# First product of seven experts: seven products of quarters in place of eight (Strassen), with the turned rows copied by two engines

## The chip, the cores and the metric

The kernel runs on one core of one Trainium2 chip. The core has five engines that run side by side and wait for each other through semaphores: TensorE (PE; the loads of its stationary operand are shown as PEld), the vector engine (DVE), the scalar engine (ACT), GpSimd (POOL) and SyncE (SP), which here only starts transfers. The metric is the time of the device for one execution, in microseconds. The kernel before takes 585.48 us (median of three runs, 585.11 to 586.97). One execution was profiled; its span, from the first to the last instruction, is 578.5 us.

## The reference

An attention block feeds a block of eight experts. Inputs are fp32, and so is all arithmetic. Only the second block is touched by the change:

```python
def _moe_ref(x, expert_emb, tau, w1, w2):         # x: 3072 x 512
    ...
    expert_idx = np.argmax(logits, axis=1)        # one of 8 experts per row
    ...
    for e in range(E):
        mask = expert_idx == e
        h = np.maximum(x[mask] @ w1[e], 0.0)      # w1[e]: 512 x 1024
        out[mask] = gate_w[mask, None] * (h @ w2[e])   # w2[e]: 1024 x 512
    return out
```

So each expert has a first product (512 by 1024), a ReLU, a second product (1024 by 512) and a factor for each row. How many rows an expert gets is known only when the kernel has computed the router.

## The kernel before

The attention part and the router take about the first 220 us. They end with tables in memory that say, for each expert, which rows are its own. What follows is the expert stage, eight rounds of `expert` called from the main function, written out for e = 0 to 7. The order of instructions on every engine is that of the program: the code asks for a manual schedule on all engines.

An expert is handled transposed. `load_rows` reads the row numbers (`emt`), casts them on DVE (`ids`, L877) and gathers up to 512 rows with GpSimd (`xg`, L881). `turn_rows` transposes them on TensorE, 16 transposes of 128 x 128 in four groups, each group into one bank of the pool `work`; DVE copies each group to `xT` (L895). `xT` holds 4 blocks of the 512 inner elements, with the rows of x along its free axis.

The number of rows is rounded up to one of 13 widths w (128, then 160 to 512 in steps of 32). For each width the code has a copy of the work, an "arm", and `tc.Switch` sends every engine to its arm by a branch (the Switch is at L957). The branch comes once per expert and engine. Ahead of it `take_width` has loaded the index into each engine's registers (L1002).

In an arm, the first product (L968) goes through the 8 blocks of 128 hidden elements, two at a time into the two banks of a tile of the pool `big` (two such tiles). Each block takes 4 matmuls, one per inner block, with a 128 x 128 piece of w1 as the stationary operand and w columns of `xT` moving. ACT applies the ReLU to both banks at once and writes them to `hT` (L970). Then `turn_rows` transposes the rows of the next expert, and the second product follows: `second` for each full group of 128 rows (L904, 16 records in the profile, 8 matmuls in the code; a bank of `work`), `second_part` for a remainder of 64 or 32 rows (L939). DVE scales each result with the gate into `y` (L907, L942) and GpSimd scatters it to the output. The group 0 comes last, outside the arm, into a bank of its own (`work0`); so TensorE has work while the engines leave an arm and reach the next one.

Weights: two sets of buffers alternate. SyncE starts w1 of expert e+1 when the first product of expert e−1 is over, and its w2 when the second product of expert e−1 is over, which is when expert e begins. The first 256 rows of expert 0 are handled during the attention part, so that expert 0 has only 160 columns left in this stage. Experts 1 to 7 have 320, 512, 320, 352, 384, 480 and 384 columns.

Of the kernel before, what the change touches and what calls it, by code (L numbers as in the profile page):

```python
# [9 lines left out]
F32 = mybir.dt.float32  # L10
# [10 lines left out]
P = 128  # L21
# [867 lines left out]
def turn_rows(k, rows, xT):  # L889

    for j, xg in enumerate(rows[2]):
        ps = k.work.tile([P, k.NC, P], F32, name="work", tag="work")
        for c in range(k.NC):
            k.nc.tensor.transpose(ps[:, c, :], xg[:, c * P : (c + 1) * P], k.ident[:])  # L894
        k.nc.vector.tensor_copy(out=xT[:, :, j * P : (j + 1) * P], in_=ps[:])  # L895


def second(k, rows, hT, w2, j, pool):

    nc = k.nc  # L900
    mt, ids, _ = rows
    ps = pool.tile([P, k.DM], F32, name="work", tag="work")
    for f in range(k.NF):
        nc.tensor.matmul(ps[:], lhsT=hT[:, f, j * P : (j + 1) * P], rhs=w2[:, f, :],  # L904
                         start=f == 0, stop=f == k.NF - 1)
    y = k.yp.tile([P, k.DM], F32, name="y", tag="y")
    nc.vector.tensor_scalar_mul(y[:], ps[:], mt[:, j, 2:3])  # L907
    nc.gpsimd.indirect_dma_start(  # L908
        out=k.out[:, :], out_offset=bass.IndirectOffsetOnAxis(ap=ids[:, j, 1:2], axis=0),
        in_=y[:], in_offset=None, bounds_check=k.N - 1, oob_is_err=False,  # L910
    )


def part_rows(k, rows, base, size):


    nc, mt, n = k.nc, rows[0], P // size
    j, p = base // P, base % P
    ids = k.rp.tile([P, 1], I32, name="pids", tag="pids")
    gate = k.rp.tile([P, 1], F32, name="pgate", tag="pgate")  # L920
    for i in range(n):
        at = slice(i * size, (i + 1) * size)
        nc.vector.tensor_scalar(out=ids[at], in0=mt[p : p + size, j, 1:2], scalar1=float(n), scalar2=float(i),
                                op0=ALU.mult, op1=ALU.add)
        nc.vector.tensor_copy(out=gate[at], in_=mt[p : p + size, j, 2:3])
    return base, size, ids, gate
# [19 lines left out]
    )  # L946


def expert(k, rows, xT, w1, w2, width=None, coming=None, behind=None):


    nc, tc = k.nc, k.tc
    hT = k.hp.tile([P, k.NF, CAP], F32, name="hT", tag="hT")
    if coming:
        coming.xT = k.xtp.tile([P, k.NC, CAP], F32, name="xT", tag="xT")
    arms = [len(WIDTHS) - 1] if width is None else tc.Switch(width.index, len(WIDTHS), hint=width.hint)
    for arm in arms:  # L957
        w = WIDTHS[arm]
        parts = []
        for size in (64, 32):  # L960
            if w % (2 * size) >= size:
                parts.append(part_rows(k, rows, w // (2 * size) * 2 * size, size))
        for f2 in range(k.NF // 2):
            ps = k.big.tile([P, 2, CAP], F32, name="big", tag="big")
            for i in range(2):
                f = 2 * f2 + i
                for c in range(k.NC):
                    nc.tensor.matmul(ps[:, i, 0:w], lhsT=w1[:, c, f * P : (f + 1) * P], rhs=xT[:, c, 0:w],  # L968
                                     start=c == 0, stop=c == k.NC - 1)
            nc.scalar.activation(hT[:, 2 * f2 : 2 * f2 + 2, 0:w], ps[:, :, 0:w], AF.Relu)  # L970
        if coming:
            turn_rows(k, coming.rows, coming.xT)
        for part in parts:
            second_part(k, part, hT, w2)
        for j in range(0 if behind else 1, w // P):
            second(k, rows, hT, w2, j, k.work)
    if coming:
        coming.width = take_width(k, coming.e)
    if behind:
        behind()  # L980
    else:
        second(k, rows, hT, w2, 0, k.work0)
# [16 lines left out]
def take_width(k, e):  # L999

    t = Net()
    v = k.nc.values_load(k.pick[0:1, e : e + 1], engines=ARMS, min_val=0, max_val=len(WIDTHS) - 1)  # L1002
    t.index, t.hint = {eng: v for eng in ARMS}, "expert%d" % e
    k.tc.switch_hint(t.index, len(WIDTHS), t.hint)  # L1004
    return t
# [62 lines left out]
def expert_pools(k, ctx):  # L1068
    def pool(name, bufs):
        return ctx.enter_context(k.tc.tile_pool(name=name, bufs=bufs, reuse_waits="tile"))  # L1070

    k.gp, k.xgp, k.xtp = pool("gp", 3), pool("xgp", 6), pool("xtp", 2)
    k.hp, k.yp, k.rp = pool("hp", 2), pool("yp", 4), pool("rp", 4)


@with_exitstack
def kernel(
    ctx: ExitStack,
    tc: tile.TileContext,
    q: bass.AP,  # L1080
    k: bass.AP,
    v: bass.AP,
    n_global: bass.AP,
    n_local: bass.AP,
    moe_expert_emb: bass.AP,
    moe_tau: bass.AP,
    moe_w1: bass.AP,
    moe_w2: bass.AP,
    out: bass.AP,
):  # L1090
    n = Net()
    n.tc, n.nc = tc, tc.nc
    nc = n.nc
    n.q, n.k, n.v, n.w1, n.w2, n.out = q, k, v, moe_w1, moe_w2, out
    n.emb_in, n.tau = moe_expert_emb, moe_tau
    n.B, n.H, n.S, n.D = q.shape
    n.E, n.DM, n.F = moe_w1.shape
    n.N = n.B * n.S
    n.NT, n.NC, n.NF = n.S // P, n.DM // P, n.F // P
    n.scale = 1.0 / math.sqrt(n.D)  # L1100
    n.slopes = [2.0 ** (-8.0 * (h + 1) / n.H) for h in range(n.H)]
    assert tuple(out.shape) == (n.N, n.DM) and n.DM == n.H * n.D == 512 and n.H == 8
    assert n.D == 64 and n.NT == 6 and n.F % (2 * P) == 0 and n.N % CAP == 0 and n.S == NB * BLK

    n.const = ctx.enter_context(tc.tile_pool(name="const", bufs=1))
    n.x_dram = tc.dram_tile([n.N + 1, n.DM], F32, name="x_dram")
    n.SL = n.N + CAP
    n.ZR = n.N - n.S
    n.meta = tc.dram_tile([n.E * n.SL, 3], F32, name="meta")
    n.c_dram = tc.dram_tile([1, n.E * (n.N // CAP) * 2], I32, name="c_dram")  # L1110
    n.scatters = []

    n.n_global, n.n_local = n_global, n_local
    with ExitStack() as moe:
        wp_a = moe.enter_context(tc.tile_pool(name="wp_a", bufs=1))
        n.w = [new_weights(n, wp_a)]
        def second_weights():
            n.wp_b = moe.enter_context(tc.tile_pool(name="wp_b", bufs=1, side="right", reuse_waits="tile"))
            return n.wp_b

        n.second_weights = second_weights
        n.ea = moe.enter_context(tc.tile_pool(name="ea", bufs=1))
        n.ea2 = moe.enter_context(tc.tile_pool(name="ea2", bufs=FIRST // P))
        with tc.manual_schedule(engines=ORDERED), ExitStack() as inner:
            window_attention(n, inner)

        n.work = ctx.enter_context(tc.tile_pool(name="work", bufs=3, space=PSUM, reuse_waits="tile"))
        n.work0 = ctx.enter_context(tc.tile_pool(name="work0", bufs=1, space=PSUM, reuse_waits="tile"))
        n.big = ctx.enter_context(tc.tile_pool(name="big", bufs=2, space=PSUM, reuse_waits="tile"))
        expert_pools(n, moe)  # L1130

        def prepare(e):
            t = Net()
            t.e = e
            at = e * n.SL
            if e == 0:
                at = nc.values_load(n.si[0:1, 0:1], engines=(SP,), min_val=0, max_val=FIRST)
            t.rows = load_rows(n, n.meta[bass.ds(at, CAP), :], n.gp, n.xgp)
            if e < 2:
                t.w = n.w[e]  # L1140
            else:
                t.w = new_weights(n, (wp_a, n.wp_b)[e % 2])
                load_weights(n, e, t.w)
            return t

        with tc.manual_schedule(engines=ORDERED | set(ARMS)):
            choose_widths(n)
            coming = prepare(0)
            coming.width = take_width(n, 0)
            second(n, n.first.rows, n.first.hT, n.w[0][1], 0, n.work)  # L1150
            coming.xT = n.xtp.tile([P, n.NC, CAP], F32, name="xT", tag="xT")
            turn_rows(n, coming.rows, coming.xT)
            for e in range(n.E):
                now, coming = coming, prepare(e + 1) if e + 1 < n.E else None
                behind = None
                if e == 0:
                    def behind():
                        second(n, n.first.rows, n.first.hT, n.w[0][1], 1, n.work0)
                expert(n, now.rows, now.xT, *now.w, now.width, coming, behind)
    n.scatters = None  # L1160
    leftover(n)

# [27 lines left out]
```

## Time and profile before

| engine | busy, us | share of the span |
|---|---|---|
| PE | 548.2 | 95% |
| PEld | 350.8 | 61% |
| DVE | 164.5 | 28% |
| ACT | 142.3 | 25% |
| POOL | 101.8 | 18% |

| lines | what | records | busy, us |
|---|---|---|---|
| L968 | first product | 512 | 159.0 |
| L904 | second product, full groups | 320 | 139.4 |
| L939 | second product, parts | 320 | 20.4 |
| L894 | transposes of rows | | 2.0 to 2.1 per expert |
| L970 | ReLU on ACT | 32 | 24.9 |
| L895 | copies of turned rows on DVE | 32 | 20.1 |
| L907 | scaling of y on DVE | 22 | 16.5 |

One matmul of the code in fp32 is two records in the profile, each with a load of its stationary operand. A record of TensorE includes its way through the array, so that the mean duration of a record (472 ns for L968) is more than the distance from one start to the next. A line of the timeline gives the start in us from the start of the span, the duration of the merged records in us, engine, line, operation, what is written from what, shape and number of records; in brackets stands the idle time of the engine just before, and what ended it. "issue" there means that the engine waited for nothing that the profile shows. In a line of a table by stretches of time there are, for each engine, busy time and number of records, then the granted clock of TensorE, the share of DMA and its rate.

### The profile page before, as it was taken

To read this page: it belongs to the slowest core of one execution; us is meant where nothing else is said; L and a number is where in the kernel's file an instruction comes from. 1 tells how busy PE (TensorE), PEld (TensorE's weight loads), DVE (VectorE), ACT (ScalarE), POOL (GpSimd) and SP (SyncE) were. 2 spreads that over 40 slices of the span, in tenths; PEclk is the share of its full clock that TensorE was granted. 3 is DMA by queue.
4 is the path that set the end of the run, shared out by engine and by line. 5 is a ranking of instruction groups with operands and counts; after the bars stand their busy time and mean duration, and the time that the engine had idled before them with its cause. 6 is when DMAs were issued, how large, how long until landed. Compare 5 with 4: busy or idle time off the path is not lost.

```text
span 578.5 us, 9188 instructions
## 1 busy us (share of the span) xinstructions
PE 548.2 (95%) x3542; PEld 350.8 (61%) x3542; DVE 164.5 (28%) x411; ACT 142.3 (25%) x336; POOL 101.8 (18%) x130
## 2 busy tenths in 40 slices
PE   8899999999989798999999999999999999999980
PEld 8577788787767676757444447556556444645530
DVE  3254666675775412111000110212101110210010
ACT  4575756756643210001001001001001001001100
POOL 2000015013232225140130013030130130110010
PEclk9799999999989898999999999999999999999995
DMA  8999998994246414543460326443461460010000
GB/s 174 194 186 201 258 254 182 256 235 72 74 128 185 126 25 129 189 150 115 177 238 0 123 84 238 158 142 120 160 232 39 159 226 30 16 43 20 2 36 25
DMA packets 117331, 78.11 MB, mean 135 GB/s; under 512 B 92965, under 2 KB 101157, under 8 KB 117169
## 3 DMA queue, kind: packets, MB, share of 16 engines
q1 hardware_dynamic: 109744, 60.72, 40.9%
q0 software_dynamic: 5536, 15.25, 7.4%
q8 instruction: 51, 0.84, 0.6%
q14 instruction: 112, 0.91, 0.5%
q10 hardware_dynamic: 1888, 0.40, 0.4%
HBM read 63.38 MB, written 13.16 MB: 132 GB/s over the span
## 4 chain that ended last, share of the span: by engine, by line
PE 58%; issue 2%; DMA 1%; POOL 1%; DVE 0%; POOLq 0%
PE big L968 27%; PE work L904 25%; PE work L939 3%; PE work L894 2%; DMA xg<-x_dram,ids 1%; POOL xg L881 0%; POOL out_dram L908 0%; POOL meta L245 0%; DVE y L907 0%; POOLq L1004 0%; DVE flags L1018 0%; POOLq L908 0%; POOLq L881 0%
## 5 line engine op out<-in xcount | busy, mean ns | idle before, releaser
L968 PE MATMUL big<-xT,w1t 128*128 128x320 f32 (+5 forms) x512 | 159.0, 472 | 0.0
L904 PE MATMUL work<-w2t,hT 128*128 128x512 f32 x320 | 139.4, 595 | 0.0
L968 PEld LDWEIGHTS big<-xT,w1t 128*128 128x128 f32 x512 | 95.0, 193 | 64.4 <-issue 31.6
L904 PEld LDWEIGHTS work<-w2t,hT 128*128 128x128 f32 x320 | 60.3, 190 | 74.6 <-issue 73.8
L970 ACT ACTIVATE hT<-big 128x640 f32<-128x640 f32 (+5 forms) x32 | 24.9, 777 | 303.7 <-PE big L968 303.7
L429 DVE TENSOR_TENSOR ex<-ex,table 126x768 f32<-126x768 f32 x64 | 57.7, 904 | 57.9 <-ACT ex L422 55.9
L907 DVE TENSOR_SCALAR y<-work,emt 128x512 f32<-128x512 f32 x22 | 16.5, 751 | 156.7 <-PE work L904 150.0
L422 ACT ACTIVATE ex<-pa 126x384 f32<-126x384 f32 (+1 forms) x128 | 53.3, 476 | 28.8 <-PE pa L418 28.8
L908 POOL DMA_INDIRECT out_dram<-y,ids x22 | 21.8, 992 | 185.6 <-DVE y L907 133.1
L895 DVE COPY xT<-work 128x512 f32<-128x512 f32 x32 | 20.1, 683 | 109.9 <-PE work L894 109.9
L418 PE MATMUL pa<-qT,kT 64*126 64x192 f32 (+1 forms) x512 | 50.7, 336 | 0.4 <-ACT ex L422 0.4
L444 PE MATMUL od<-ex,v 126*64 126x192 f32 (+1 forms) x576 | 48.6, 316 | 0.0
L418 PEld LDWEIGHTS pa<-qT,kT 64*126 64x126 f32 x512 | 41.5, 190 | 10.7 <-issue 6.0
L444 PEld LDWEIGHTS od<-ex,v 126*64 126x64 f32 x576 | 36.0, 142 | 8.8 <-issue 4.7
L881 POOL DMA_INDIRECT xg<-x_dram,ids x34 | 33.3, 981 | 23.0 <-issue 15.6
L245 POOL DMA_INDIRECT meta<-mt,slot x24 | 26.3, 1095 | 38.3 <-DVE good L542 7.8
L452 PE MATMUL od<-ex,halves 126*32 126x192 f32 (+1 forms) x576 | 26.9, 310 | 0.0
L943 POOL DMA_INDIRECT out_dram<-y,pids x7 | 7.1, 1015 | 89.3 <-DVE y L942 84.0
L217 POOL TENSOR_TENSOR ss<-ss,half 128x3 f32<-128x3 f32 (+1 forms) x6 | 6.3, 1047 | 93.0 <-ACT junk L526 93.0
L526 ACT ACTIVATE junk<-xs 128x512 f32<-128x512 f32 x24 | 15.2, 632 | 27.1 <-DVE xs L521 22.2
L939 PE MATMUL work<-w2t,hT 128*32 128x128 f32 (+1 forms) x320 | 20.4, 317 | 0.0
L452 PEld LDWEIGHTS od<-ex,halves 126*32 126x32 f32 x576 | 14.9, 111 | 8.8 <-issue 3.6
(143 smaller groups left out, 389.9 us busy)
## 6 DMA issues: line engine op xcount, KB each, us to landing
w1t<-in_moe_w_dram SPq DMA_DIRECT2D x6, 2048.0 KB, 9.5
w2t<-in_moe_w_dram SPq DMA_DIRECT2D x6, 2048.0 KB, 11.5
v<-in_v_dram SPq DMA_DIRECT2D x32, 192.0 KB, 4.7
x_dram<-xs SPq DMA_DIRECT2D x24, 256.0 KB, 2.8
k<-in_k_dram SPq DMA_DIRECT2D x28, 192.0 KB, 4.0
q<-in_q_dram SPq DMA_DIRECT2D x28, 192.0 KB, 4.2
w1t<-in_moe_w_dram SPq DMA_DIRECT2D x32, 128.0 KB, 3.7
w2t<-in_moe_w_dram SPq DMA_DIRECT2D x32, 128.0 KB, 3.7
```

Of the source, the lines that this page charges most:

```text
L245: i = nc.gpsimd.indirect_dma_start(out=k.meta[:], out_offset=bass.IndirectOffsetOnAxis(ap=slot[:, t : t + 1], axis=0), in_=mt[:, t, :], in ...
L418: nc.tensor.matmul(u.sp[e][0:ROWS, a * n : (a + 1) * n], lhsT=t.kT[rows, j, 0:ROWS], rhs=t.qT[rows, j * BLK : j * BLK + n], start=True, st ...
L422: nc.scalar.activation(u.ex[:, e], u.sp[e][0:ROWS, 0 : 2 * u.n].rearrange("p (a c) -> p a c", a=2), AF.Exp, scale=k.scale)
L429: nc.vector.tensor_tensor(out=exv, in0=exv, in1=tab[:, :, 0 : u.n // BLK, :], op=ALU.mult)
L444: nc.tensor.matmul(g.od[a][e * D : (e + 1) * D, at : at + c1 - c0], lhsT=g.v[0:ROWS, 2 * a + e, u.j, :], rhs=u.ex[:, e, a, c0:c1], start=f ...
L452: nc.tensor.matmul(g.od[2][32 * i : 32 * i + 32, at : at + c1 - c0], lhsT=k.halves[0:ROWS, g.m].rearrange("p i c -> p (i c)"), rhs=u.ex[:, ...
L881: nc.gpsimd.indirect_dma_start(out=xg[:], out_offset=None, in_=k.x_dram[0 : upto or k.N + 1, :], in_offset=bass.IndirectOffsetOnAxis(ap=id ...
L904: nc.tensor.matmul(ps[:], lhsT=hT[:, f, j * P : (j + 1) * P], rhs=w2[:, f, :], start=f == 0, stop=f == k.NF - 1)
L908: nc.gpsimd.indirect_dma_start(out=k.out[:, :], out_offset=bass.IndirectOffsetOnAxis(ap=ids[:, j, 1:2], axis=0), in_=y[:], in_offset=None, ...
L939: nc.tensor.matmul(ps[i * size : (i + 1) * size, 0:m], lhsT=hT[:, f, base : base + size], rhs=w2[:, f, i * m : (i + 1) * m], start=f == 0, ...
L968: nc.tensor.matmul(ps[:, i, 0:w], lhsT=w1[:, c, f * P : (f + 1) * P], rhs=xT[:, c, 0:w], start=c == 0, stop=c == k.NC - 1)
L970: nc.scalar.activation(hT[:, 2 * f2 : 2 * f2 + 2, 0:w], ps[:, :, 0:w], AF.Relu)
```

## The change

For experts 1 to 7, where the width is at least 256, the first product is no longer computed as eight products of quarters (two halves of the inner axis, two of the hidden axis, two of the rows) but as seven, by Strassen's scheme in Winograd's form. With A the quarters of w1, B those of `xT`, the seven left factors are three quarters of w1 and four sums of quarters (`sums`); the right factors are three quarters of `xT` and four differences (`dif`). The seven products, added up in the right way, give the four quarters of the hidden layer. Each product has 8 matmuls of the code with n = w/2 columns. It is done in two halves (`go`), one call of `product` each: 4 matmuls, 8 records of the profile, into one bank, which takes n columns of two hidden blocks. A bank that is used twice accumulates a second product upon the first.

The purpose is fewer columns for TensorE to stream. In return the other engines have more to do:

- DVE makes the four differences of `xT` at the start of the arm (`t1` to `t4`), five sums of a bank and a piece in SBUF for each half (`u2`, `u3` and three that are written to `hT`), and, once per expert, the four sums of the next expert's w1 (`weight_sums`, after the copies of the turned rows and ahead of the gates of the parts).
- ACT copies the first product of each half (`p1`) and applies the ReLU in eight pieces; six of them in place on `hT`, after DVE's sum.
- In `turn_rows` the copies of the groups 1 and 3 go to ACT, for all experts.
- What `second_part` needs of small values (`part_rows`) is computed after the first product instead of ahead of it, when the seven products are used.

```diff
@@ turn_rows
-        k.nc.vector.tensor_copy(out=xT[:, :, j * P : (j + 1) * P], in_=ps[:])
+        eng = k.nc.scalar.copy if j % 2 else k.nc.vector.tensor_copy
+        eng(out=xT[:, :, j * P : (j + 1) * P], in_=ps[:])
@@ new functions
+def weight_sums(k, w1, sums):
...
+    two(0, a(1, 0), a(1, 1), ALU.add)
+    two(1, sums[:, 0], a(0, 0), ALU.subtract)
+    two(2, a(0, 0), a(1, 0), ALU.subtract)
+    two(3, a(0, 1), sums[:, 1], ALU.subtract)
...
+def first_by_seven(k, xT, w1, sums, hT, w):
...
+    t1 = two(0, b(0, 1), b(0, 0))
+    t2 = two(1, b(1, 1), t1)
+    t3 = two(2, b(1, 1), b(0, 1))
+    t4 = two(3, b(1, 0), t2)
...
+    def product(ps, left, right, go, first):
+        for f in range(2):
+            for c in range(K):
+                nc.tensor.matmul(ps[:, f], lhsT=left[:, c, (2 * go + f) * P : (2 * go + f + 1) * P], rhs=right[:, c],
+                                 start=first and f == 0 and c == 0, stop=True, skip_group_check=True)
...
+    one = banks()
+    p1 = [new("p1") for go in range(2)]
+    for go in range(2):
+        product(one[go], a(0, 0), b(0, 0), go, True)
+        nc.scalar.copy(out=p1[go], in_=one[go])
+    for go in range(2):
+        product(one[go], a(0, 1), b(1, 0), go, False)
+        relu(h(0, 0, go), one[go])
+    keep = None
+    for go in range(2):
+        if go == 0:
+            p6, p7 = banks()
+        u2, u3 = new("u2"), new("u3")
+        if go == 1:
+            p6 = keep
+            p7, p5 = banks()
+        product(p6, sums[:, 1], t2, go, True)
+        add(u2, p1[go], p6)
+        product(p7, sums[:, 2], t3, go, True)
+        add(u3, u2, p7)
+        if go == 0:
+            p5, keep = banks()
+        product(p5, sums[:, 0], t1, go, True)
+        add(h(1, 1, go), u3, p5)
+        relu(h(1, 1, go), h(1, 1, go))
+        product(p7, a(1, 1), t4, go, False)
+        add(h(1, 0, go), u2, p7)
+        relu(h(1, 0, go), h(1, 0, go))
+        product(p5, sums[:, 3], b(1, 1), go, False)
+        add(h(0, 1, go), u2, p5)
+        relu(h(0, 1, go), h(0, 1, go))
@@ expert, in the arm
-        parts = []
-        for size in (64, 32):
-            if w % (2 * size) >= size:
-                parts.append(part_rows(k, rows, w // (2 * size) * 2 * size, size))
-        for f2 in range(k.NF // 2):
...
+        if sums is not None and w >= 2 * P:
+            first_by_seven(k, xT, w1, sums, hT, w)
+        else:
+            parts = arm_parts(k, rows, w)
+            first_by_eight(k, xT, w1, hT, w)
         if coming:
             turn_rows(k, coming.rows, coming.xT)
+            weight_sums(k, coming.w[0], coming.sums)
+        if not parts:
+            parts = arm_parts(k, rows, w)
```

`first_by_eight` is the first product as it was. There is one tile `sums` for all experts. Expert 0 gets no sums and keeps the first product of before.

More of the change, by code (lines that the diff above doesn't have):

```diff
@@ L946, in second_part, with arm_parts, first_by_eight @@
     )
-def expert(k, rows, xT, w1, w2, width=None, coming=None, behind=None):
+def arm_parts(k, rows, w):
+    return [part_rows(k, rows, w // (2 * size) * 2 * size, size) for size in (64, 32) if w % (2 * size) >= size]
+def first_by_eight(k, xT, w1, hT, w):
+    nc = k.nc
+    for f2 in range(k.NF // 2):
+        ps = k.big.tile([P, 2, CAP], F32, name="big", tag="big")
+        for i in range(2):
+            f = 2 * f2 + i
+            for c in range(k.NC):
+                nc.tensor.matmul(ps[:, i, 0:w], lhsT=w1[:, c, f * P : (f + 1) * P], rhs=xT[:, c, 0:w],
+                                 start=c == 0, stop=c == k.NC - 1)
+        nc.scalar.activation(hT[:, 2 * f2 : 2 * f2 + 2, 0:w], ps[:, :, 0:w], AF.Relu)
@@ new lines, in new_sums, with a, two @@
+def new_sums(k, pool):
+    return pool.tile([P, 4, k.NC // 2, k.F // 2], F32, name="sums")
+def weight_sums(k, w1, sums):
+    nc, K, M = k.nc, k.NC // 2, k.F // 2
+    def a(m, n):
+        return w1[:, n * K : (n + 1) * K, m * M : (m + 1) * M]
+    def two(i, x, y, op):
+        nc.vector.tensor_tensor(out=sums[:, i], in0=x, in1=y, op=op)
+    two(0, a(1, 0), a(1, 1), ALU.add)
+    two(1, sums[:, 0], a(0, 0), ALU.subtract)
+    two(2, a(0, 0), a(1, 0), ALU.subtract)
+    two(3, a(0, 1), sums[:, 1], ALU.subtract)
@@ new lines, in first_by_seven, with b, two, a @@
+def first_by_seven(k, xT, w1, sums, hT, w):
+    nc, K, M, n = k.nc, k.NC // 2, k.F // 2, w // 2
+    F2 = k.NF // 2
+    dif = k.sp.tile([P, 4, K, CAP // 2], F32, name="dif", tag="dif")
+    def b(i, j):
+        return xT[:, i * K : (i + 1) * K, j * n : (j + 1) * n]
+    def two(i, x, y):
+        nc.vector.tensor_tensor(out=dif[:, i, :, 0:n], in0=x, in1=y, op=ALU.subtract)
+        return dif[:, i, :, 0:n]
+    t1 = two(0, b(0, 1), b(0, 0))
+    t2 = two(1, b(1, 1), t1)
+    t3 = two(2, b(1, 1), b(0, 1))
+    t4 = two(3, b(1, 0), t2)
+    def a(m, i):
+        return w1[:, i * K : (i + 1) * K, m * M : (m + 1) * M]
+    def banks():
+        t = k.big.tile([P, 2, CAP], F32, name="big", tag="big")
+        return [t[:, i, 0:w].rearrange("p (f s) -> p f s", f=2) for i in range(2)]
+    def product(ps, left, right, go, first):
[3 more added lines that the diff above has]
+                                 start=first and f == 0 and c == 0, stop=True, skip_group_check=True)
+    def h(m, j, go):
+        f = m * F2 + 2 * go
+        return hT[:, f : f + 2, j * n : (j + 1) * n]
+    def add(out, x, y):
+        nc.vector.tensor_tensor(out=out, in0=x, in1=y, op=ALU.add)
+    def relu(out, x):
+        nc.scalar.activation(out, x, AF.Relu)
+    def new(name):
+        return k.sp.tile([P, 2, CAP // 2], F32, name=name, tag=name)[:, :, 0:n]
+    one = banks()
[29 more added lines that the diff above has]
+        relu(h(0, 1, go), h(0, 1, go))
@@ L952, in expert @@
+def expert(k, rows, xT, w1, w2, width=None, coming=None, behind=None, sums=None):
     nc, tc = k.nc, k.tc
@@ L959, in expert @@
         parts = []
-        for size in (64, 32):
-            if w % (2 * size) >= size:
-                parts.append(part_rows(k, rows, w // (2 * size) * 2 * size, size))
-        for f2 in range(k.NF // 2):
[L964 to L970, printed above, removed]
+        if sums is not None and w >= 2 * P:
[3 more added lines that the diff above has]
+            first_by_eight(k, xT, w1, hT, w)
         if coming:
             turn_rows(k, coming.rows, coming.xT)
+            weight_sums(k, coming.w[0], coming.sums)
+        if not parts:
+            parts = arm_parts(k, rows, w)
         for part in parts:
@@ L1072, in expert_pools @@
     k.gp, k.xgp, k.xtp = pool("gp", 3), pool("xgp", 6), pool("xtp", 2)
-    k.hp, k.yp, k.rp = pool("hp", 2), pool("yp", 4), pool("rp", 4)
+    k.hp, k.yp, k.rp, k.sp = pool("hp", 2), pool("yp", 4), pool("rp", 4), pool("sp", 2)
 @with_exitstack
@@ L1149 @@
             coming.width = take_width(n, 0)
+            coming.sums, sums = None, new_sums(n, moe.enter_context(tc.tile_pool(name="sums", bufs=1)))
             second(n, n.first.rows, n.first.hT, n.w[0][1], 0, n.work)
@@ L1155 @@
                 behind = None
+                if coming:
+                    coming.sums = sums
                 if e == 0:
@@ L1158, in behind @@
                         second(n, n.first.rows, n.first.hT, n.w[0][1], 1, n.work0)
-                expert(n, now.rows, now.xT, *now.w, now.width, coming, behind)
+                expert(n, now.rows, now.xT, *now.w, now.width, coming, behind, now.sums)
     n.scatters = None
```

## The prediction

> **What bounds the kernel now.** I read the slices of the span first, then the chain that ended last, then TensorE's timeline over the expert stage, and last the vector engine around each start of an expert.
>
> ```profile
> PE   8899999999989798999999999999999999999980
> PEclk9799999999989898999999999999999999999995
> PE 58%; issue 2%; DMA 1%; POOL 1%; DVE 0%; POOLq 0%
> ```
>
> From slice 16 on (230 us) TensorE is busy without a break, at full clock, and the chain runs through it alone: 27% of it is the first product (L968), 25% the second (L904). What TensorE saves there, the kernel saves, if nothing new makes it wait. TensorE's timeline for experts 3 to 7:
>
> ```profile
> 346.73 17.39 PE L968 MATMUL big<-xT,w1t 128*128 128x320 f32 x64
> 383.38 19.10 PE L968 MATMUL big<-xT,w1t 128*128 128x352 f32 x64
> 423.62 20.80 PE L968 MATMUL big<-xT,w1t 128*128 128x384 f32 x64
> 467.01 25.92 PE L968 MATMUL big<-xT,w1t 128*128 128x480 f32 x64
> 520.95 20.80 PE L968 MATMUL big<-xT,w1t 128*128 128x384 f32 x64
> ```
>
> Each of the code's 32 matmuls shows as two records. Experts 1 and 2 have widths 320 and 512, expert 0 has 160. No engine makes TensorE wait inside these products. The vector engine at the start of expert 6 (467.01), from its timeline (start, duration, engine, instruction, idle before):
>
> ```profile
> 467.21 0.75 DVE L907 TENSOR_SCALAR y<-work,emt 128x512 f32<-128x512 f32 x1 [6.12 <-PE work L904]
> 467.88 0.16 DVE L877 CAST ids<-emt 128x8 int32<-128x8 f32 x1
> 473.67 0.14 DVE L923 TENSOR_SCALAR pids<-emt 64x1 int32<-64x1 f32 x1 [5.63 <-issue]
> ```
>
> This is the reading on which all below turns. DVE scales the last rows of the expert before, casts the ids, takes the Switch's branch, and then waits for nothing that the profile shows for 5.63 us before the first instruction of its arm. At 467.2 SyncE starts the 2 MB load of the next w2. At expert 0, with no weight load, the same gap is 2.43 us. Now it costs nothing: DVE has no work for the first product. The records of L957 give DVE's arrival in the arm, after the expert's first matmul: 4.66, 5.35, 6.20, 6.68, 6.09, 6.57 and 3.53 us for experts 1 to 7 (no weights are loaded at the last).
>
> **What the Trainium skill says.** *TensorE: Matmul & The Clock Gate*, Back-to-back issue gap: N/2.4 + 2.5 ns warm. The trace agrees, at two passes a record: expert 0's 160-column records start 136 ns apart from 229 us on (320/2.4 + 2.5), expert 5's 384-column ones 322 ns. The 190 ns that a weight load takes there does not set the pace. *Runtime: NRT & Kernel Launch*, Instruction fetch mechanics: a taken branch to a page that is not held forces a fetch by DMA first. The gaps of 2.43 to 5.75 us marked "issue" after the Switch agree, and grow where the w2 load begins just ahead. *TensorE*, Part 1: after an idle window of some 3.4 us the clock is halved until a busy one. This view (us, busy of PE, PEld, DVE, ACT, POOL, then the clock) agrees:
>
> ```profile
> 220.80:224.20 3.40, 1.28 (x8) 0.84 (x8) 2.27 (x4) 0.00 (x0) 1.02 (x1) 1.00 0.78 202
> 224.20:227.60 3.40, 3.13 (x12) 2.88 (x13) 0.77 (x2) 0.00 (x0) 0.48 (x1) 0.50 0.05 18
> ```
>
> *VectorE: DVE Perf Modes*, errata section: an fp32 tensor_tensor takes (N+151)/0.96 ns; the trace has 549 ns at 384 elements (557 by the formula).
>
> **The change, part by part.** *Products.* 64 records of w columns become 112 of n = w/2. A record costs 2 x columns/2.4 + 2.5 ns, so an expert saves 6.667 ns x w − 0.12 us. Experts 1 to 7 have 320+512+320+352+384+480+384 = 2752 columns: 18.35 − 0.84 = **−17.5 us**. Expert 0 stays.
>
> *The new wait.* The first four calls of product need only xT and w1. They last 32 records: 4.35 us at n=160, 4.77 at 176, 5.20 at 192, 6.48 at 240, 6.91 at 256. The fifth call (p6) needs t2, DVE's second difference, and DVE's differences are the first instructions of its arm. So TensorE stands until arrival + 0.09 (hint to first instruction, as before) + two tensor_tensors of 2n elements + 0.03 (gap of dependent ones, L321 to L322) + 0.06 (DVE's end to TensorE, L895 to L894). The duration is read between the rows of 192 elements (352 ns) and 384 (549): 0.48, 0.52, 0.55, 0.65, 0.68 us. Expert 1: 4.66+0.18+0.97 = 5.81, less 4.35: 1.46 us. Expert 2: 6.89 against 6.91: 0. Expert 3: 7.35 − 4.35 = 3.00. Expert 4: 7.89 − 4.77 = 3.12. Expert 5: 7.37 − 5.20 = 2.17. Expert 6: 8.04 − 6.48 = 1.56. Expert 7: 4.81 against 5.20: 0. Sum **+11.3 us**. Behind the waiting matmul stand all the expert's other products; TensorE runs them in order. I take the arrivals as they are, since branch, fetch and w2 load stay where they were. With an undisturbed fetch at every expert (3.5 us, as at expert 7) the stall is 0.3 us at experts 1, 3 and 4 or less, 1 us in all. With one more line of instructions to be fetched within the longer arm it is some 3 us more.
>
> *Clock.* A stall of 3 us nearly fills a window of 3.4. A halved window costs 3.4/2 = 1.7 us. The trace halves the clock after a window with 1.28 us of TensorE work; slices with 70% and more passed. Experts 3, 4 and perhaps 5 are near the line; I take 1.3 windows, **+2.2 us**, between 0 and five windows (8.5).
>
> *Inside the loop.* A call lasts 8 records, 1.09 to 1.73 us; a sum on DVE 0.5 to 0.7 us plus 0.2 for the signal. Every bank that is reused (p7, p5) has a whole call between its reader and its next matmul, and DVE's five sums in a round take 2.5 to 3.4 us beside 5.4 to 8.6 of TensorE. I price these waits at nothing; so also ACT's copies of p1 and its halved ReLUs (0.44 us at 320 elements from 437 ns): ACT reaches its arm long before TensorE (L957: 453.7 for the expert that starts at 467.0).
>
> *The end of the product.* The last sum and ReLU now come after the last matmul. DVE's add (0.5 to 0.7 us) stands ahead of the copy of the first turned rows, and ACT's ReLU ahead of the second copy. TensorE's fourth group of transposes needs the first copy's bank: copied at 0.2+0.6+0.68 = 1.5 us instead of 1.3 after the product. I take 0.25 us at experts 1 to 6, **+1.5**. Expert 7 has no transposes: its second product runs 4 records (0.87 us) and waits for the last ReLU at 0.2+0.55+0.05+0.5+0.1 = 1.4: **+0.5**.
>
> *Hidden.* weight_sums: four times (1024+151)/0.96 = 1.22 us by the skill's formula, about 5 us on DVE after the copies. Queued behind it are the gates and the scaling of y; TensorE meanwhile has parts and second products of 10 us and more, with three banks, and the sums are wanted an expert later. The next w1 was loaded during the expert before (w1 is issued at 274.21 and 326.32, lands in 9.5 us). ACT's two copies of turned rows cost nothing and bring nothing: they fall into idle time.
>
> Sum: 585.5 − 17.5 + 11.3 + 2.2 + 1.5 + 0.5 = **583.5 us**.
>
> **The rivals.** *DVE in time:* the fetch ends sooner, for instance because the arms lie otherwise in the instruction lines. Then 585.5 − 17.5 + 1 + 2 = **571 us**. Against it: all six middle experts show the gap. For it: 2.4 us at expert 0. *Stalls and clock:* every stall halves a window, five at 1.7 = 8.5 in place of 2.2, and a fetch inside a longer arm adds up to 3: 590 to 593, say **590 us**, slower than before. For it: nothing is known between 1.28 us and about 2.4 us of work in a window. Against it: the window must catch most of the stall. *Weight loads set the pace at half width:* 190 ns a record at n below 226 would add 54, 54, 41, 27.5 and 27.5 ns x 112 at experts 1, 3, 4, 5, 7 = 23 us: **606 us**. Against it: 136 ns measured at 160 columns.
>
> **How the numbers follow.** Forecast as worked out 0.57 (580 to 587 with zero to three halved windows), DVE in time 0.14, stalls and clock 0.26, weight loads 0.03. The likeliest gives 583.5; its neighbours reach from 573, a fetch half as disturbed, to 591. Faster by over 0.3% (below 583.7): the 0.14 and 0.34 of the forecast. Within: 0.20 of it and 0.03 of the third. Slower: the rest.
>
> **What would show it.** TensorE's records of products 160 wide at 136 ns; after 32 records of an expert a gap of 1.5 to 3 us at experts 1, 3, 4, 5, 6, ended by DVE's differences; none at 2 and 7; DVE's "issue" idle of 4 to 6 us ahead of the differences; one or two 3.4 us stretches at clock 0.5 behind those gaps. No gap there would make me wrong towards 571, half clock behind each of them towards 590.

## The result, and the profile after

The changed kernel takes 620.34 us (median of four runs, 618.77 to 623.97), the kernel before on the same chip 585.3 us. The ratio is 1.0603, with a 95% interval of 1.0548 to 1.0658: 35.0 us slower. The forecast was 583.5 us, 2.0 us below the 585.5 it started from, with neighbours from 573 to 591.

First the slices of TensorE and its granted clock over the changed kernel's span (617.4 us), then the shares of its chain of waits:

```profile
PE   9899999979989889979888988988988988997890
PEclk9899999998989899999999999999999999999995
...
PE 52%; issue 4%; DVE 4%; ACT 1%; DMA 1%; POOL 0%; DVEq 0%; POOLq 0%; ACTq 0%
```

In the expert stage the unbroken row of nines has become a row of eights and nines: TensorE is held up a little everywhere and nowhere long. The clock is as full as before (0.978 on average, 0.971 before), so half speed isn't the cause. The chain, which had next to no DVE or ACT work in it (0%), now has 4% of the one and 1% of the other: TensorE waits for them by turns. TensorE's timeline of expert 5, which before was the one line `423.62 20.80`, shows where (L1018 is the matmul of `product`, L1026 the sum on DVE, L1029 the ReLU and L1038 the copy to `p1`):

```profile
447.98 1.46 PE L1018 MATMUL big<-xT,w1t 128*128 128x192 f32 x8
450.06 1.57 PE L1018 MATMUL big<-xT,w1t 128*128 128x192 f32 x8 [0.61 <-ACT p L1038]
452.24 1.57 PE L1018 MATMUL big<-xT,w1t 128*128 128x192 f32 x8 [0.61 <-ACT p L1038]
454.39 1.57 PE L1018 MATMUL big<-xT,w1t 128*128 128x192 f32 x8 [0.58 <-ACT hT L1029]
455.79 1.46 PE L1018 MATMUL big<-dif,sums 128*128 128x192 f32 x8
457.97 2.87 PE L1018 MATMUL big<-dif,sums 128*128 128x192 f32 x16 [0.72 <-issue]
460.68 1.46 PE L1018 MATMUL big<-dif,w1t 128*128 128x192 f32 x8
461.98 1.46 PE L1018 MATMUL big<-xT,sums 128*128 128x192 f32 x8
464.09 2.87 PE L1018 MATMUL big<-dif,sums 128*128 128x192 f32 x16 [0.65 <-DVE hT L1026]
467.60 1.57 PE L1018 MATMUL big<-dif,sums 128*128 128x192 f32 x8 [0.65 <-DVE u L1026]
469.82 1.57 PE L1018 MATMUL big<-dif,w1t 128*128 128x192 f32 x8 [0.65 <-DVE hT L1026]
472.03 1.57 PE L1018 MATMUL big<-xT,sums 128*128 128x192 f32 x8 [0.65 <-DVE hT L1026]
473.43 2.07 PE L894 MATMUL work<-ident,xg 128*128 128x128 f32 x16
```

Eight records are one call of `product`, and at full pace one call starts 8 x 162.5 ns = 1.30 us after the other. That is so at the calls 8 and 9 (460.68 to 461.98), which wait for nothing. Before eight of the fourteen calls (2, 3, 4, 6, 10, 12, 13, 14) TensorE stands, and the call starts 2.1 to 2.2 us after the one before it. The gap that the prediction was about, ahead of the fifth call (455.79), isn't there.

From the first record to the transposes expert 5 takes 473.43 − 447.98 = 25.45 us; at full pace it would be 112 x 162.5 ns = 18.20. So 7.25 us are lost. The same subtraction at experts 1 to 7 gives 6.66, 8.24, 7.44, 7.51, 7.25, 7.99 and 7.25, together 52.3 us. The balance is −17.5 + 52.3 = +34.8 us, and 35.0 were measured. Nothing else of size is left to look for.

Whom does TensorE wait for? The chain of semaphores, summed for its weight loads (idle us, times, longest):

```profile
PEld big L1018 <- DVE hT L1026: 20.1, 21, 1.2
PEld big L1018 <- ACT p L1038: 12.8, 14, 1.1
PEld big L1018 <- DVE u L1026: 12.0, 12, 1.3
PEld big L1018 <- ACT hT L1029: 6.2, 7, 1.1
```

Those are the readers of the banks: DVE's sums (`hT`, `u`) and ACT's copies and ReLUs, three waits for ACT and four or five for DVE in each of seven experts. These figures are idle time of the weight loader, which holds its ordinary pauses too; the losses above are from starts. (Call 6 of expert 5, at 457.97, has "issue" as its releaser; at expert 7, which has the same width, the profile names DVE's `u`.)

Now the second call. It is the clearest case, because it writes into a bank that nothing has used before in this expert. The one instruction of ACT beside it, from ACT's timeline:

```profile
449.53 0.48 ACT L1038 COPY p<-big 128x384 f32<-128x384 f32 x1 [20.18 <-PE big L1018]
```

This copy reads what the first call left in `one[0]`. It ends at 450.01. The second call, into `one[1]`, starts at 450.06. It needs no result of the copy and doesn't touch its bank. What the two banks share is the tile: `banks()` asks the pool for one tile of two banks and hands out slices. All eight waits are of this kind. Call 3 goes into `one[0]`, whose copy ended long ago (450.01), but starts 50 ns after the copy of `one[1]` (451.71 + 0.48 = 452.19); call 6 fills `p7` and waits for the sum that reads `p6`, its neighbour in the tile. The calls without a wait are those in a fresh tile (5, 7, 11) or whose neighbour's reader is done (8, 9).

One such wait costs, at call 2: the way of the last record through the array 0.16, signal 0.09, copy 0.48, signal 0.05: 0.78 us. Later ones cost 0.1 more, since a call that follows a wait is itself longer (1.57 instead of 1.46). Over all widths a wait costs 0.7 us (call 2 of expert 1) to 1.05 us (call 13 of expert 2): the reader has more columns to read there (a copy to `p1` takes 0.42 us at expert 1 and 0.58 at expert 2).

### The profile page after: what moved, and what is told of

It reads as the page before. It is cut to its first block, busy times and chain, and to the rows that moved or that the text cites. A ratio compares the mean times of both kernels' runs of the same rounds, so it can differ in the third digit from the quotient of the medians.

```text
span 617.4 us, 10087 instructions
## 1 busy us (share of the span) xinstructions
PE 545.1 (88%) x3878; PEld 388.9 (63%) x3878; DVE 241.1 (39%) x521; ACT 164.8 (27%) x394; POOL 102.2 (17%) x130
## 4 chain that ended last, share of the span: by engine, by line
PE 52%; issue 4%; DVE 4%; ACT 1%; DMA 1%; POOL 0%; DVEq 0%; POOLq 0%; ACTq 0%
PE work L905 24%; PE big L1018 22%; PE work L940 3%; PE work L894 2%; DVE hT L1026 2%; PE big L963 1%; DVE u L1026 1%; ACT p L1038 1%; DMA xg<-x_dram,ids 1%; ACT hT L1029 0%; DVE dif L1000 0%; POOL xg L881 0%; POOL out_dram L909 0%; POOL meta L245 0%; DVE y L908 0%
## 5 line engine op out<-in xcount | busy, mean ns | idle before, releaser
L1018 PE MATMUL big<-dif,sums 128*128 128x160 f32 (+4 forms) x336 | 62.8, 337 | 15.0 <-DVE u L1026 8.3
L1018 PEld LDWEIGHTS big<-dif,sums 128*128 128x128 f32 x336 | 53.7, 190 | 23.4 <-DVE u L1026 12.0
L1018 PE MATMUL big<-xT,w1t 128*128 128x160 f32 (+4 forms) x224 | 44.0, 339 | 12.7 <-ACT p L1038 8.6
L1029 ACT ACTIVATE hT<-hT 128x320 f32<-128x320 f32 (+4 forms) x42 | 22.3, 531 | 109.3 <-DVE hT L1026 109.3
L1018 PEld LDWEIGHTS big<-xT,w1t 128*128 128x128 f32 x224 | 35.9, 190 | 23.3 <-ACT p L1038 12.8
L1038 ACT COPY p<-big 128x320 f32<-128x320 f32 (+4 forms) x14 | 6.8, 486 | 162.4 <-PE big L1018 162.4
L444 PE MATMUL od<-ex,v 126*64 126x192 f32 (+1 forms) x576 | 49.9, 322 | 0.0
L1026 DVE TENSOR_TENSOR hT<-u,big 128x320 f32<-128x320 f32 (+4 forms) x42 | 23.7, 564 | 51.6 <-PE big L1018 51.6
L1018 PE MATMUL big<-xT,sums 128*128 128x160 f32 (+4 forms) x112 | 21.6, 336 | 4.6 <-DVE hT L1026 4.6
```

What stands on the lines that cost most here:

```text
L444: nc.tensor.matmul(g.od[a][e * D : (e + 1) * D, at : at + c1 - c0], lhsT=g.v[0:ROWS, 2 * a + e, u.j, :], rhs=u.ex[:, e, a, c0:c1], start=f ...
L1018: nc.tensor.matmul(ps[:, f], lhsT=left[:, c, (2 * go + f) * P : (2 * go + f + 1) * P], rhs=right[:, c], start=first and f == 0 and c == 0, ...
L1026: nc.vector.tensor_tensor(out=out, in0=x, in1=y, op=ALU.add)
L1029: nc.scalar.activation(out, x, AF.Relu)
```

## The experiments

The theory after this: the program waits for a tile, not for a bank, and the change is the first code here that gives the two banks of a `big` tile readers of their own. The rival: seven products have true dependencies that cost this in any case (sums that are too slow, banks that are reused too soon). A third reading lays the loss on DVE's and ACT's added work. Two sets of four kernels ran; each set has its own runs of the kernel before (579.70 us median in the first, 587.53 in the second, on two other chips). The second set has the two kernels with the ReLU taken apart, and the late load on the changed kernel and on the kernel before; the first has the other four. So ratios are compared, and "in us of the first chip" is ratio x 585.3.

**One bank to a tile.** The calls, their order and the sums stay. Four tiles of one bank stand in place of two tiles of two. (Expert 0 and the leftover path, which shares the pool, are fitted to this; expert 0's ReLU goes by bank.)

```diff
-        t = k.big.tile([P, 2, CAP], F32, name="big", tag="big")
-        return [t[:, i, 0:w].rearrange("p (f s) -> p f s", f=2) for i in range(2)]
+        t = [k.big.tile([P, CAP], F32, name="big", tag="big") for i in range(2)]
+        return [x[:, 0:w].rearrange("p (f s) -> p f s", f=2) for x in t]
...
-        n.big = ctx.enter_context(tc.tile_pool(name="big", bufs=2, space=PSUM, reuse_waits="tile"))
+        n.big = moe.enter_context(tc.tile_pool(name="big", bufs=4, space=PSUM, reuse_waits="tile"))
```

> The changed kernel with every bank of the first product as a tile of its own (four tiles of one bank in place of two of two banks; the eight-product path applies its ReLU bank by bank). Theory 1 (the waits of the changed kernel are between the two banks of one tile: a matmul into one bank waits for the reader of the other): the gaps of 0.5 to 0.85 us before the calls of product go, 52 us in all; what stays is the wait for DVE's differences, 0 to 3.2 us an expert, 11 us in all. Time 579 to 585 us. Rival A (the chain product, sum, product is itself too slow for two rounds of banks): the gaps stay, 612 us or more. Rival B (the vector engine's added work holds TensorE up): 605 to 620 us.

Measured: 577.32 us, ratio 0.9971 (0.9951 to 0.9991). In us of the first chip that is 583.6. The eight waits are gone. TensorE's timeline of expert 5:

```profile
425.39 5.36 PE L1023 MATMUL big<-xT,w1t 128*128 128x192 f32 x32
433.03 4.17 PE L1023 MATMUL big<-dif,sums 128*128 128x192 f32 x24 [2.28 <-DVE dif L1005]
437.04 1.46 PE L1023 MATMUL big<-dif,w1t 128*128 128x192 f32 x8
438.34 1.46 PE L1023 MATMUL big<-xT,sums 128*128 128x192 f32 x8
439.64 4.06 PE L1023 MATMUL big<-dif,sums 128*128 128x192 f32 x24
443.54 1.46 PE L1023 MATMUL big<-dif,w1t 128*128 128x192 f32 x8
444.84 1.46 PE L1023 MATMUL big<-xT,sums 128*128 128x192 f32 x8
```

The first four calls run as one line of 32 records, the other ten follow each other without a wait, and between the two stands the wait that the prediction had: TensorE for DVE's differences. DVE's timeline there:

```profile
426.26 0.16 DVE L877 CAST ids<-emt 128x8 int32<-128x8 f32 x1
431.83 0.56 DVE L1005 TENSOR_TENSOR dif<-xT 128x384 f32<-128x384 f32 x1 [5.41 <-ACT hT L1034]
432.42 0.56 DVE L1005 TENSOR_TENSOR dif<-xT,dif 128x384 f32<-128x384 f32 x1
```

DVE is idle for 5.41 us between the cast and the first difference. (The releaser named, a ReLU on ACT, writes nothing that the first difference reads: that needs only `xT`, which was copied during the expert before.) Over all experts the waits say:

```profile
PEld big L1023 <- DVE dif L1005: 12.6, 6, 3.2
```

By expert, against full pace, 1.76, 0.66, 6.23, 2.97, 2.55, 1.28 and 0 us are lost, 15.45 in all; −17.5 + 15.45 = −2.0, and the medians differ by −2.4. At expert 3 the loss is not the wait alone. This view by stretches (us, busy of PE, PEld, DVE, ACT, POOL, then the clock) covers it:

```profile
347.00:350.40 3.40, 1.06 (x8) 0.82 (x7) 0.51 (x1) 0.87 (x2) 2.49 (x4) 1.00 0.95 327
350.40:353.80 3.40, 2.80 (x10) 2.80 (x11) 1.51 (x5) 0.00 (x0) 0.44 (x1) 0.50 1.04 410
353.80:357.20 3.40, 3.40 (x14) 3.40 (x14) 0.78 (x2) 0.00 (x0) 0.00 (x0) 0.50 0.48 155
```

After a stretch with 1.06 us of TensorE work the clock is at half for two stretches. In the second of them 14 records fill 3.4 us; at full pace they take 14 x 136 ns = 1.9. The fifth call starts at 351.00, where full pace would have had it at 343.55 + 4.35 = 347.90. So of the 6.23 us 3.1 are the wait and 3.1 are lost behind it, while the clock is at half.

So the eight waits came from the tile: none of them is left. Of the true dependencies only the wait for the differences costs time, which the changed kernel had hidden behind the others. The rival falls. So does the third reading: all of DVE's and ACT's added work is in this kernel too, and its time is that of the kernel before.

**The same readers without the seven products.** If the tile is the cause, the kernel before must show it too as soon as each bank of its tile gets a reader of its own. This takes its one ReLU for two banks apart:

```diff
-        nc.scalar.activation(hT[:, 2 * f2 : 2 * f2 + 2, 0:w], ps[:, :, 0:w], AF.Relu)
+            nc.scalar.activation(hT[:, f, 0:w], ps[:, i, 0:w], AF.Relu)
```

> The kernel before, its products as they were, with the ReLU applied to each bank right after that bank's matmuls, in place of once per tile of two banks. Theory 1 (a matmul into one bank of a tile waits for the reader of its other bank): four waits an expert, each the way through the array plus one ReLU of 0.3 to 0.6 us, 0.6 to 0.95 us in all, over eight experts 26 us: ratio to before 1.040 to 1.048. If the waits of the changed kernel came from the seven products themselves: ratio 0.998 to 1.003.

And this is the same with a tile for each bank (the pool then has four tiles of one bank in place of two of two):

```diff
-        ps = k.big.tile([P, 2, CAP], F32, name="big", tag="big")
         for i in range(2):
+            ps = k.big.tile([P, CAP], F32, name="big", tag="big")
```

> As relu_bank_two, but each bank is a tile of its own. Theory 1: no waits, ratio to before 0.997 to 1.003. If the smaller ReLUs themselves hold TensorE up: the same as relu_bank_two.

Measured: with two banks to a tile 613.81 us, ratio 1.0458 (1.0425 to 1.0491); with one bank to a tile 587.69 us, ratio 1.0000 (0.9983 to 1.0018). TensorE's timeline of expert 5, first with two banks to a tile:

```profile
446.35 2.74 PE L968 MATMUL big<-xT,w1t 128*128 128x384 f32 x8
449.73 5.43 PE L968 MATMUL big<-xT,w1t 128*128 128x384 f32 x16 [0.64 <-ACT hT L970]
455.74 5.43 PE L968 MATMUL big<-xT,w1t 128*128 128x384 f32 x16 [0.58 <-ACT hT L970]
...
467.76 2.85 PE L968 MATMUL big<-xT,w1t 128*128 128x384 f32 x8 [0.58 <-ACT hT L970]
```

and with one:

```profile
430.86 20.80 PE L968 MATMUL big<-xT,w1t 128*128 128x384 f32 x64
```

ReLUs, products and banks are the same in both. The second bank of each tile waits for the ReLU of the first, four times an expert. From start to start 16 records take 6.01 us in place of 16 x 322 ns = 5.16: 0.85 us for a wait. Eight experts with four waits of 0.8 to 0.9 are 26 to 29 us, and 26.3 were measured (613.81 − 587.53). This has nothing of Strassen in it.

**DVE's added work alone.** The differences and the weight sums are made as in the changed kernel, but the first product is then done in eight products of quarters, as before (what DVE has made isn't used):

```diff
     t4 = two(3, b(1, 0), t2)
+    first_by_eight(k, xT, w1, hT, w)
+    return
```

> The changed kernel with the eight products of before; the differences of xT and the sums of w1 are still computed on DVE, but no product uses them; the turned rows are copied in turn. Theory 1: this work lies beside TensorE's, 584 to 588 us. Rival B: a large part of the 35 us stays, 600 us or more.

Measured: 577.84 us, ratio 0.9974 (0.9955 to 0.9993); in us of the first chip 583.8, just under the range expected. DVE's timeline after the turned rows of an expert:

```profile
444.35 1.22 DVE L981 TENSOR_TENSOR sums<-w1t 128x1024 f32<-128x1024 f32 x1
...
451.18 0.75 DVE L908 TENSOR_SCALAR y<-work,emt 128x512 f32<-128x512 f32 x1 [2.08 <-PE work L905]
```

The four sums take 1.22 us each, and DVE is idle for 2.08 us more before TensorE has the first rows to scale. This part of the added work, the differences and the weight sums, is hidden. (The sums of the banks and ACT's smaller pieces aren't in this kernel; they are in the one with one bank to a tile.)

**The turned rows alone**, in the kernel before:

```diff
-        k.nc.vector.tensor_copy(out=xT[:, :, j * P : (j + 1) * P], in_=ps[:])
+        eng = k.nc.scalar.copy if j % 2 else k.nc.vector.tensor_copy
+        eng(out=xT[:, :, j * P : (j + 1) * P], in_=ps[:])
```

> The kernel before with one part of the change: turned rows copied by DVE and ACT in turn. All theories: no effect on TensorE, 584 to 587 us.

Measured: 578.44 us, ratio 0.9981 (0.9967 to 0.9995): 0.2%, less than can be built on.

**Where DVE's late arrival comes from.** The prediction put it on the fetch of the arm's first instructions, slowed by the 2 MB load of w2 that starts at the same moment. The edit on top of one bank to a tile lets this load wait until the rows of the next expert have been gathered (SyncE's next transfer, the 6 KB of row numbers, moves back with it):

```diff
-    nc.sync.dma_start(w[1][:], k.w2[e].rearrange("(f p) m -> p f m", p=P))
+    i = nc.sync.dma_start(w[1][:], k.w2[e].rearrange("(f p) m -> p f m", p=P))
+    for g in after:
+        k.tc.add_manual_dep(i.ins, g.name,
+                            mybir.DependencyInfo(mybir.DependencyClass.Sync, mybir.DependencyReason.DATA),
+                            reason="keeps the transfer away from the branch at an expert's start")
...
-                load_weights(n, e, t.w)
+                load_weights(n, e, t.w, [n.gather.ins])
```

> As one_bank, and the load of the next w2 waits for the last gather of rows, so that it starts some 12 us after an expert's start in place of 0.2 us. If the vector engine's late arrival in its arm comes from its instruction fetch queueing behind that load, it arrives after 3 to 3.6 us at all experts and the wait for the differences falls to about 1 us in all: 569 to 574 us. If the fetch is late for another reason: the time of one_bank within 2 us.

Measured: 562.87 us (560.1 to 566.3), ratio 0.9743 (0.9685 to 0.9801), in us of the first chip 570. DVE's timeline at the start of expert 5 (411.50):

```profile
412.37 0.16 DVE L881 CAST ids<-emt 128x8 int32<-128x8 f32 x1
415.10 0.56 DVE L1009 TENSOR_TENSOR dif<-xT 128x384 f32<-128x384 f32 x1 [2.57 <-ACT p L1047]
```

The w2 load now starts at 424.28, and the idle time after the cast is 2.57 us in place of 5.41. DVE arrives 3.2 to 3.6 us after the first matmul at all seven experts, where it was up to 6.3. The loss against full pace is 0.65 us over all experts; so −17.5 + 0.65 = −16.8 us, and the medians differ by as much (562.87 − 579.70; the runs spread over 6 us, so such closeness is in part chance). This version beats both kernels.

The trace holds more on the fetch than the idle time. In both kernels, at each of the experts 1 to 7, a packet of the DMA queue that the page calls "q14 instruction" starts 1.93 to 2.05 us ahead of the first difference: at expert 5 at 429.87 with the load beside it (difference at 431.83), at 413.13 with the load put off (415.10). Counted from the expert's first matmul it starts after 3.0 to 4.5 us where the load is beside it (experts 1 to 6), and after 1.4 to 1.7 us where none is. The packet itself takes no longer at expert 5 (0.31 and 0.34 us). So if it is the fetch of DVE's first instructions, the delay lies ahead of its start and not in the transfer. The record doesn't name the engine that the packet is for.

The same edit without the other one, on the changed kernel and on the kernel before:

> The changed kernel with two-bank tiles as it is, and the load of the next w2 put off until the last gather of rows has landed. Theory 1: the waits between banks remain and had hidden most of the vector engine's late arrival; only the gaps before the first call with differences go (0.7 us at one expert, 0.5 at another): ratio to before 1.055 to 1.062. If the late fetch were the main cause: below 1.04.

> The kernel before with the load of the next w2 put off in the same way. DVE has nothing to do for the first product there, so all theories: ratio to before 0.998 to 1.002. If putting the load off is worth something by itself (so that the gain of one_bank_w2late isn't that of the seven products): below 0.99.

Measured: 621.57 us, ratio 1.0563 (1.0519 to 1.0608), and 587.71 us, ratio 1.0002 (0.9983 to 1.0022). In the changed kernel DVE now arrives after 3.2 to 3.4 us and the eight waits remain, with their time. In the kernel before nobody waits for DVE's arrival. The late load is worth 13 us (0.9971 to 0.9743) once the tiles are mended, and next to nothing otherwise: a wait that stands behind another one shows its price only when that one is gone.

## Why the prediction was wrong, step by step

**Products, −17.5 us: right.** Records of 160 columns start 136 ns apart. With both waits away, the first products of experts 1 to 7 take 15.39, 24.17, 15.58, 16.81, 18.20, 22.68 and 18.20 us; before it was 17.23, 27.47, 17.23, 18.93, 20.64, 25.76 and 20.64. The difference of the sums is 16.9. The rival of weight loads that set the pace falls.

**"Inside the loop", priced at nothing: this step failed.** It said: "Every bank that is reused (p7, p5) has a whole call between its reader and its next matmul". That is true of the banks, and the run with one bank to a tile shows that they cost nothing. But the program doesn't wait for banks. The changed kernel's waits are those of a tile of two banks, and each costs 0.7 to 1.05 us (0.8 to 0.9 at expert 5), since way through the array, signals and reader lie bare between two calls. Of the 52.3 us lost, 1.25 are what is left of the wait for the differences (experts 3 and 4, below); 8 waits x 7 experts = 56 have the other 51.1, 0.91 us apiece. The Trainium skill, in *PSUM — Partial Sum Buffer*, Terms, names the bank (by quadrants of partitions) as the place in which two engines may not meet. The runs agree: with one bank to a tile ACT and DVE read one bank while TensorE fills the next, without any wait. The wait between neighbours is therefore the program's, not the chip's. Which rule of the program layer makes it, and whether another setting of the pool would lift it, was not tried.

The kernel before couldn't show it: its one ReLU reads both banks, and TensorE is by then in the other tile. The code could: `banks()` returns two slices of one tile, and the second call follows the first into the same one. That the page of before had no wait inside L968 was taken as a sign that banks come free in time, and it meant only that no tile had a second reader.

**The wait for DVE's differences, +11.3 us: right in mechanism and size, but hidden.** With one bank to a tile it is, by the start of the fifth call, 1.65, 0.55, 3.10, 2.86, 2.44, 1.17 and 0 us at experts 1 to 7, 11.8 in all; that expert 2 waits was not foreseen. In the changed kernel the waits at the calls 2 to 4 delay the fifth call by 2.6 us at expert 5 and about as much elsewhere, and DVE's lateness runs out behind them; only experts 3 and 4 keep 0.7 and 0.5 us. The cause held as well, as far as it was tried: with the load put off the stall is gone. *Runtime: NRT & Kernel Launch*, Instruction fetch mechanics, has the fetch as a DMA of the engine's sequencer, and *DMA: Bandwidth & Descriptors*, Queues, rings and completion order (Arbitration), has the DMA engines take turns between queues a packet at a time; an arrival that comes 3 us sooner when a load is moved agrees with both. If the packets of "q14 instruction" above are DVE's, the fetch starts late and isn't slow itself; what holds it back, no trace here shows.

**Clock, +2.2 us: not in the changed kernel, 3.1 us with one bank to a tile (two stretches behind one wait).** Its short waits never empty a stretch of 3.4 us.

**End of the product, +1.5 us: nothing.** From the first transpose to the next product it is 1.91 us at expert 5 against 2.05 before, and 12.0 us over experts 1 to 6 in both kernels. DVE's add does stand ahead of the first copy (473.63, the copy at 474.11), but ACT takes the second copy meanwhile, and the weight loader waits for the fourth group's bank 0.17 us, against 0.21 before.

**Expert 7's second product, +0.5 us: nothing.** Four records of 512 columns last 4 x 429 ns = 1.72 us, not 0.87; so the last ReLU (1.4 us) is hidden.

**Hidden work: right** (0.9974 with the differences and weight sums alone, 0.9981 with the turned rows alone).

That one bank to a tile gives 583.6 us, beside a forecast of 583.5, is luck. The terms of loss were 11.3 + 2.2 + 1.5 + 0.5 = 15.5 us. The runs have 11.8 for the wait, 3.1 at half clock and 0.5 for longer first records after a wait, 15.4 together, and nothing for the two last terms: what was priced too high made up for what was priced too low. The step that failed is the one priced at nothing, and it was 51 us.

## What to carry to other kernels

Ask of every buffer what the program waits for: a tile that holds two banks with different readers makes TensorE wait for the neighbour's reader, and giving each bank a tile of its own costs no space. One reader for both banks of a tile hides such waits, since TensorE fills the other tile meanwhile; a reader for each bank lays them open, here at 0.7 to 1.05 us apiece. The first work of an engine after a branch can come late, as DVE's did here; keep large transfers away from that moment.

## What the runs showed of the hardware

- DVE was idle for 2.3 to 2.7 us across a taken branch with no large load beside it (one bank to a tile, late w2, experts 1 to 7), and for 3.9 to 5.5 us with the 2 MB load just started (one bank to a tile, experts 1 to 6). In all of these a packet of "q14 instruction" starts 1.93 to 2.05 us ahead of DVE's first work.
- A stretch of 3.4 us with 1.06 us of TensorE work was followed by two stretches at half clock, though TensorE was busy for 2.80 us of the first; the wait of 2.9 us at expert 4 was followed by none. Each is one case in one profile, and what separates the two was not tried.
- The first record after a wait lasts about 0.1 us longer than those in a row: at call 2 of expert 5 of the changed kernel 430 ns instead of 326.
